# Three PSUM banks of one score tile become two tiles, in a chunked attention with two feed-forward layers

## The chip, the cores and the metric

The kernel runs on one core of one Trainium2 chip. The metric is device time in microseconds (us) of one execution; the median of several runs is given. The core has five engines with a queue of instructions each: TensorE (PE in the profile; PEld is its weight load), VectorE (DVE), ScalarE (ACT), GpSimd (POOL) and SyncE (SP, which here only issues DMAs). Each engine works its queue in order: an instruction that waits holds up all that stand behind it.

## The reference

Three stages follow each other on 3072 tokens (4 batches of 768), 512 channels wide:

- Attention in chunks: 8 heads of 64 channels. A chunk of 32 queries sees 8 memory keys and its own 32 keys with 16 before and 8 after, cut off at the ends of the sequence. Softmax, then the product with V.
- First feed-forward layer: `h = x @ w_in` (512 to 2048), `g = max(h, 0) + alpha * min(h, 0)`, `g @ w_out` back to 512.
- Second feed-forward layer of the same sizes with `g = h * sigmoid(1.702 h)`.

The weights of the two layers and their activations are worked on as a high and a low float16 half, so that one product takes three float16 matmuls.

## The kernel before

The tokens are cut into 12 blocks of 256 (`nb`), and each block into two halves of 128 queries (`i` = 0, 1). For blocks 2 to 11 the attention of one half goes through these steps, each a function in the code:

- `att_qk` (lines 476 to 483): the scores. For each of 8 heads two matmuls of 128x160 go into the PSUM tile `sps`, which is three banks of 512 float32: heads 0 to 2 in bank 0, heads 3 to 5 in bank 1, heads 6 and 7 in bank 2.
- `att_ext` (lines 485 to 504): ACT copies the band that each chunk needs out of `sps` into the SBUF tile `sc`: one copy of the memory columns (line 497) and one for each of four groups of 32 partitions (line 499). For blocks 2 to 11 each copy takes all three banks at once, as nine heads, the ninth being empty space.
- `att_smax`, `att_exp`, `att_sum`, `att_a16`: softmax on DVE, ACT and POOL, and the split of the probabilities into two float16 halves.
- `att_ta` (line 535): a transposing DMA from the SP queue makes `aT`.
- `att_pv` (lines 537 to 549): the product with V, 48 small matmuls (128x32, line 548). Half 0 writes bank 0 of `sps`, half 1 writes bank 1.
- `att_xhi` (ACT, line 129) and `att_xlo` (DVE, line 132) read that bank and write the high and the low half of `xt`, the input of the first feed-forward layer.

Blocks 0 and 1 do the scores in float32 (`att_qk32`, line 407); for them `att_ext` already has two parts, and their product with V goes to another PSUM pool.

The first layer works on pairs of 128 hidden channels: a group of 24 matmuls of line 580 (`mlp_g1`, reads `xt`) and a group of 24 of line 660 (`mlp_g2`). From about 200 us on these alternate on PE, 192 of each to a block, and the attention of the coming block is strewn between them. The plan `ATT` gives each attention step of a block its place in half steps of this loop; but what is written there is only the order in which the program is recorded. A scheduler, which follows the dependencies and its own estimates of durations, then fixes the order on each engine, and puts in the waits between engines. It keeps count of who wrote and who read a tile.

The second layer (lines 591 and 674) begins at about 724 us and uses no attention tile; `w2_open` closes the pool of `sps` and puts three other PSUM tiles in its place.

Of the kernel before, what the change touches and what calls it, by code (L numbers as in the profile page):

```python
# [8 lines left out]
F32 = mybir.dt.float32  # L9
# [17 lines left out]
F32B = (0, 1)  # L27
# [9 lines left out]
def kernel(  # L37
# [14 lines left out]
    nc = tc.nc  # L52
    B, H, S, D = q.shape
# [7 lines left out]
    HP = H // 2  # L61
    WIN = LEFT + CH + RIGHT
    SL = WIN + NM
# [3 lines left out]
    TW = BAND + NM  # L67
# [210 lines left out]
    att = {}  # L278

    def geo(nb):  # L280
        b, j = divmod(nb, S // TB)
        return b, j * TB

    def eng(nb):
        return nc.vector if nb == 0 else nc.gpsimd
# [112 lines left out]
    def att_qk32(nb, i):  # L398
        qt, kt = att["q", nb], att["k", nb]
        k0 = 0 if i == 0 else NM + 128  # L400
        for h in range(H):
            j, a = divmod(h, 2)
            if j < HP - 1:
                o, r, w = sps[:, a, j * TW:j * TW + TW], slice(a * D, a * D + D), qt[a * D:a * D + D, i, j]
            else:
                o, r, w = sps[:, 2, a * TW:a * TW + TW], slice(0, 2 * D), qz[:, i, a]
            nc.tensor.matmul(out=o, lhsT=w, rhs=kt[r, j, k0:k0 + TW], start=True, stop=True)

    def att_xmax(nb, i):
# [66 lines left out]
    def att_qk(nb, i):  # L476
        q1, q2 = att["q", nb]
        kt = att["k", nb]
        k0 = 0 if i == 0 else NM + 128
        for h in range(H):  # L480
            o = sps[:, h // 3, h % 3 * TW:h % 3 * TW + TW]
            nc.tensor.matmul(out=o, lhsT=q1[:, i, h], rhs=kt[:, h, k0:k0 + TW], start=True, stop=False)
            nc.tensor.matmul(out=o, lhsT=q2[:, i, h], rhs=kt[:, h, k0:k0 + TW], start=False, stop=True)

    def att_ext(nb, i):
        sc = at_p.tile([128, 9, SL], F32, tag="sc", name="sc", bufs=2)
        b, t0 = geo(nb)
        t1 = t0 + 128 * i
        sv = sc.rearrange("p (a b) s -> p a b s", a=3)
        pv = sps[:, :, 0:3 * TW].rearrange("p a (b t) -> p a b t", b=3)  # L490
        mo = 0 if i == 0 else BAND
        bo = NM if i == 0 else 0
        parts = [(sv, pv)]
        if nb in F32B:
            parts = [(sc[:, 0:6].rearrange("p (b a) s -> p a b s", a=2), pv[:, 0:2]), (sc[:, 6:8], pv[:, 2, 0:2])]
        for d, x in parts:
            nc.scalar.copy(d[..., WIN:SL], x[..., mo:mo + NM])
            for c in range(4):
                nc.scalar.copy(d[32 * c:32 * c + 32, ..., 0:WIN], x[32 * c:32 * c + 32, ..., bo + CH * c:bo + CH * c + WIN])  # L499
        if t1 == 0:  # L500
            eng(nb).memset(sc[0:32, 0:H, 0:LEFT], NEG)
        if t1 + 128 == S:
            nc.gpsimd.memset(sc[96:128, 0:H, WIN - RIGHT:WIN], NEG)
        att["s", nb, i] = sc[:, 0:H]

    def att_smax(nb, i):
        sc = att["s", nb, i]
# [30 lines left out]
    def att_pv(nb, i):  # L538
        aT = att.pop(("a", nb, i))
        if i == 0:  # L540
            xt[nb] = xt_p.tile([128, 2, KT, TB], F16, tag="xt", name="xt")
        xp = sps[:, i].rearrange("p (j t) -> p j t", j=HP)
        for j in range(HP):
            for c in range(4):
                o = xp[:, j, 32 * c:32 * c + 32]
                w = vbd[:, 4 * i + c, j].rearrange("p a (d t) -> p (a d) t", t=2)
                for n, (wt, a) in enumerate(((0, 0), (1, 0), (0, 1))):
                    nc.tensor.matmul(out=o, lhsT=w[:, :, wt], rhs=aT[:, a, j, 32 * c:32 * c + 32], start=(n == 0), stop=(n == 2))  # L548
        att["xp", nb, i] = xp
# [282 lines left out]
    def run_plan(t):  # L832
# [12 lines left out]
        (14, att_hi, 2), (15, att_lo, 2), (16, att_vw), (13, att_swap),  # L845
        *[(17 + h // 2, att_vr, h) for h in range(H)],
        (18, att_qk, 0), (18, att_ext, 0), (20, att_smax, 0), (21, att_qk, 1), (21, att_ext, 1),
        (22, att_exp, 0), (23, att_smax, 1), (24, att_sum, 0), (25, att_exp, 1), (26, att_a16, 0),
        (27, att_sum, 1), (28, att_ta, 0), (29, att_a16, 1), (31, att_ta, 1),
        (32, att_pv, 0), (33, att_xhi, 0), (34, att_xlo, 0), (34, att_pv, 1), (35, att_xhi, 1), (36, att_xlo, 1),  # L850
    ]
    for nb in range(3, NB):
# [3 lines left out]
    def split(m, p):  # L856
# [4 lines left out]
        (-103, zero_k), (-100.91, att_load, 0, 1), (-98.84, att_load, 0, 0), (-96.77, att_t32, 0),  # L861
        (-96.06, zero_v), (-95.87, alpha_load), (-95.35, att_load, 1, 0), (-90.2, w_load, 0, 1),
        (-89.08, alpha_prep), (-85.94, att_qk32, 0, 0), (-84.86, w_load, 0, 0), (-82.33, att_v32, 0, 1),
        (-78.47, w_load, 1, 0), (-74.28, w_max, 0, 0), (-68.89, att_ext, 0, 0), (-58.71, att_qk32, 0, 1),
        (-54.62, att_ext, 0, 1), (-47.58, att_smax, 0, 0), (-45.32, att_exp, 0, 0), (-41.66, att_sum, 0, 0),
        (-34.37, w_all, 0, 0, 1), (-33.6, w_max, 0, 1), (-31.58, w_scale, 0, 0, 1), (-28.74, att_v32, 0, 0),
        (-28.07, att_load, 1, 1), (-27.6, att_smax, 0, 1), (-26.72, w_all, 0, 1, 2), (-25.47, att_exp, 0, 1),
# [9 lines left out]
        (-7.61, w_dec_a, 0, 2), (-7.5, w_dec_b, 0, 2), (-7.25, w_dec_b, 0, 1), (-7.2, w_load, 1, 5),  # L877
        (-6.9, w_max, 0, 4), (-6.52, att_max, 2, 0), (-6.51, att_xlo, 0, 1), (-5.97, w_max, 1, 1),
        (-5.96, att_qk32, 1, 0), (-4.67, w_split_a, 0, 1), (-4.66, w_max, 1, 0), (-3.68, att_max, 2, 2),
        (-2.76, att_max, 2, 1), (-2.32, w_dec_a, 0, 3), (-2.14, w_split_a, 0, 2), (-1.65, w_split_b, 0, 1),  # L880
        (-1.25, att_ext, 1, 0), (-1.23, att_smax, 1, 0), (-0.54, att_exp, 1, 0), (-0.03, att_sum, 1, 0),
# [9 lines left out]
        (8.68, att_lo, 2, 2), (8.89, att_tq, 2), (8.99, w_first), (9.35, w_dec_b, 1, 0),  # L891
        (9.5, att_xlo, 1, 0), (9.66, att_xhi, 1, 1), (9.8, att_vw, 2), (9.83, w_dec_a, 1, 3),
        (10.76, att_swap, 2), (10.94, att_qk, 2, 0), (11.19, att_xlo, 1, 1), (11.28, att_vr, 2, 1),
        (12.17, w_max, 0, 6), (13.48, w_load, 0, 7), (13.76, att_ext, 2, 0), (14.12, w_dec_b, 1, 1),
        (14.26, att_smax, 2, 0), (14.44, w_dec_b, 1, 3), (14.78, att_vr, 2, 7), (14.88, w_max, 0, 5),
        (15.48, att_exp, 2, 0), (15.76, w_max, 0, 7), (16.07, w_split_a, 1, 1), (16.29, att_qk, 2, 1),
        (16.29, att_sum, 2, 0), (17.48, att_ext, 2, 1), (18.83, w_split_b, 1, 1), (18.86, att_smax, 2, 1),
        (18.99, att_vr, 2, 5), (19.25, w_all, 0, 4, 6), (19.27, w_split_a, 1, 0), (20.02, w_max, 1, 5),
# [4 lines left out]
        (25.09, att_vr, 2, 2), (25.62, w_split_b, 1, 0), (26.74, att_ta, 2, 0), (26.89, w_scale, 0, 6, 8),  # L903
        (27.59, att_a16, 2, 1), (28.18, w_load, 1, 4), (29.46, w_max, 1, 4), (29.5, w_split_a, 0, 4),
        (29.59, att_pv, 2, 0), (30.52, w_scale, 1, 4, 6), (30.65, att_ta, 2, 1), (31.18, w_dec_a, 0, 7),
        (31.7, w_split_b, 1, 2), (31.87, att_xhi, 2, 0), (32.19, att_pv, 2, 1), (33.03, w_dec_a, 0, 6),
        (33.15, w_split_b, 0, 4), (33.67, w_dec_b, 0, 7), (33.84, w_dec_b, 0, 6), (34.16, att_xhi, 2, 1),
        (34.77, w_split_a, 0, 6), (35.75, att_xlo, 2, 1), (35.88, att_xlo, 2, 0), (36.25, w_dec_b, 0, 5),
# [10 lines left out]
    for g in range(NP):  # L919
        m, p = 2 + g % 2, g // 2  # L920
        t = 24 * (g + 3) - 8 + EX3
# [12 lines left out]
    for b in range(NB):  # L934
        t = 3 * ((NP * (b + 1) if b >= NA else HF * (NA + b + 1)) + L0) + 2 - 3
# [7 lines left out]
    for sb in range(NB // 2):  # L943
        t = Q0 + 48 * sb
# [3 lines left out]
        t = 48 * sb + 80 if sb else 101.5  # L948
# [3 lines left out]
        if sb == NB // 2 - 1:  # L952
            t = Q0 + 20
# [8 lines left out]
    ps_s = l1.enter_context(tc.tile_pool(name="ps_s", bufs=1, space=PSUM))  # L962
    w_p = l1.enter_context(tc.tile_pool(name="wdec", bufs=2))
    at_1 = l1.enter_context(tc.tile_pool(name="at1", bufs=1))
    at_p = l1.enter_context(tc.tile_pool(name="at", bufs=1))
# [2 lines left out]
    vf = at_1.tile([128, 3, H, D], F32, name="vf")  # L968
    vbd = at_1.tile([128, 8, HP, 2, 2 * D], F16, name="vbd")
    lazy["yl_p"] = w_p  # L970
    sps = ps_s.tile([128, 3, 512], F32, name="sps")
    pend = []
    act = []

# [43 lines left out]
    qz = ident[:, 0:512].rearrange("p (i a t) -> p i a t", i=2, a=2)  # L1018
    ident = eye
    nc.vector.memset(wv, 0.0)  # L1020
    nc.vector.memset(sps[:, 2], 0.0)
    nc.scalar.activation(out=wv[:, 8:9], in_=wv[:, 7:8], func=ACTF.Exp)
    run_plan(0)
    for s in range(STEPS + EX):
# [3 lines left out]
    for q in range(STEPS // 2 + LQ):  # L1028
        t = Q0 + 6 * q
# [21 lines left out]
        if xs:  # L1051
            sb, p = divmod(q, NP)
# [33 lines left out]
```

## Time and profile before

| | |
|---|---|
| median of 3 runs | 1192.45 us (1189.9 to 1194.58) |
| profiled execution, first to last instruction | 1188.6 us |
| PE busy | 1079.9 us (91%) |
| DVE, POOL, ACT busy | 854.5 (72%), 639.9 (54%), 633.0 us (53%) |
| DMA queue with nearly all bytes | 51.0% of 16 engines |

The page of the profiled execution gives its span and no other time of its own; the median of the runs is 3.85 us above that span. The span falls into a start, in which PE is busy about three quarters of the time (up to some 200 us), the first layer with the attention beside it (to 724 us) and the second layer, in which PE hardly ever stops. A row of the timeline has start and duration in us, engine, line, operation, output and inputs with their shapes, the count of instructions merged into it, and in brackets how long the engine stood idle before it and what ended that.

### The profile page before, as it was taken

How to read it: one execution, taken by the hardware profiler on the slowest of the kernel's cores; microseconds unless marked ns; L12 is line 12 of the kernel's file. 1: busy time of each engine (PE TensorE's matmuls, PEld its weight loads, DVE VectorE, ACT ScalarE, POOL GpSimd, SP SyncE). 2: the span in 40 equal slices, each digit the busy share in tenths (PEclk: the TensorE clock that was granted, in tenths of full speed). 3: DMA queues.
4: the chain of work that ended last, by engine and by line, in shares of the span. 5: the costliest groups of instructions: out<-in, count | busy, mean ns of one | idle time of the engine just before them, and what ended most of it. 6: DMA issues, size and time to landing. Idle time of an engine off the chain costs nothing.

```text
span 1188.6 us, 25661 instructions
## 1 busy us (share of the span) xinstructions
PE 1079.9 (91%) x10294; PEld 957.4 (81%) x10294; DVE 854.5 (72%) x1509; ACT 633.0 (53%) x968; POOL 639.9 (54%) x740
## 2 busy tenths in 40 slices
PE   4676788988989898999799999989999999999998
PEld 3665677977878787888698988878888888888887
DVE  6899995659778777858797634787676767667662
ACT  4567455556666476656665632545444444443442
POOL 1244542218666456617572811787685676666672
PEclk9668998999999899999899999999999999999999
DMA  9969328576999678888966380640110202000001
GB/s 203 308 126 194 90 72 172 83 145 180 228 219 257 136 203 172 229 151 197 191 184 139 108 345 19 266 170 19 58 41 6 76 19 80 20 6 14 19 19 37
DMA packets 250536, 154.53 MB, mean 130 GB/s; under 512 B 201200, under 2 KB 221680, under 8 KB 249392
## 3 DMA queue, kind: packets, MB, share of 16 engines
q1 hardware_dynamic: 250416, 152.88, 51.0%
q8 instruction: 81, 1.33, 0.5%
q14 instruction: 39, 0.32, 0.1%
HBM read 91.96 MB, written 38.93 MB: 110 GB/s over the span
## 4 chain that ended last, share of the span: by engine, by line
PE 50%; DVE 20%; DMA 11%; POOL 5%; issue 5%; ACT 5%; SPq 3%; ACTq 0%; POOLq 0%; DVEq 0%
PE acc L674 17%; PE x L591 16%; PE h L580 8%; PE acc L660 7%; DVE g L132 3%; DVE gf L618 2%; DMA q<-q 2%; POOL ga L625 2%; DVE wmax L126 2%; DMA wbig<-in_moe_w_in_dram 2%; DVE wr L200 1%; DMA kf<-in_k_dram 1%; DMA qf<-in_q_dram 1%; DMA w<-in_moe_w_in_dram 1%; DVE wr L201 1%
## 5 line engine op out<-in xcount | busy, mean ns | idle before, releaser
L625 POOL TENSOR_TENSOR ga<-ga 128x128 f32<-128x128 f32 x384 | 213.2, 580 | 172.2 <-DVE ga L623 160.1
L580 PE MATMUL h<-xt,wbig 128*128 128x256 f16 x2304 | 280.7, 280 | 21.0 <-ACT xt L129 15.0
L660 PE MATMUL acc<-g,wbig 128*128 128x256 f16 x2304 | 279.9, 279 | 13.1 <-DVE gf L618 6.2
L580 PEld LDWEIGHTS <-wbig 128*128 128x128 f16 x2304 | 230.9, 100 | 53.9 <-issue 22.6
L660 PEld LDWEIGHTS <-wbig 128*128 128x128 f16 x2304 | 229.3, 100 | 44.3 <-DVE gf L618 7.3
L674 PE MATMUL acc<-w2o,g 128*128 128x256 f16 x2016 | 231.6, 274 | 4.2 <-ACT g L129 3.4
L591 PE MATMUL x<-yt,w2i 128*128 128x256 f16 x2016 | 229.9, 273 | 0.9 <-DVE ha L601 0.9
L674 PEld LDWEIGHTS <-g 128*128 128x128 f16 x2016 | 197.4, 98 | 29.1 <-ACT g L129 4.4
L591 PEld LDWEIGHTS <-w2i 128*128 128x128 f16 x2016 | 197.4, 98 | 24.1 <-issue 1.1
L132 DVE SCALAR_TENSOR_TENSOR g<-ga,gk,g 128x896 f16<-128x896 f32 x96 | 121.1, 1267 | 91.0 <-ACT g L129 90.7
L129 ACT ACTIVATE g<-ga,gk 128x896 f16<-128x896 f32 x96 | 98.9, 1037 | 96.0 <-POOL ga L625 87.1
L618 DVE SCALAR_TENSOR_TENSOR gf<-t,oma,h 128x256 f32<-128x256 f32 x192 | 83.4, 472 | 75.0 <-ACT t L615 74.9
L615 ACT ACTIVATE t<-h 128x512 f32<-128x512 f32 x96 | 56.7, 591 | 66.8 <-PE h L580 38.8
L132 DVE SCALAR_TENSOR_TENSOR g<-gf,gk,g 128x512 f16<-128x512 f32 x81 | 77.8, 960 | 17.0 <-ACT g L129 16.7
L808 POOL TENSOR_TENSOR o<-o 128x256 f32<-128x256 f32 x77 | 74.4, 980 | 10.0 <-ACT o L803 9.5
L622 ACT ACTIVATE ga<-ha,l2t 128x512 f32<-128x512 f32 x48 | 34.4, 718 | 80.7 <-DVE ha L603 80.7
L230 POOL TENSOR_TENSOR wt<-wr 128x512 f32<-128x512 f32 x16 | 24.0, 1500 | 81.2 <-DVE wr L207 59.0
L216 POOL TENSOR_TENSOR wbig<-wr,wbig 128x1024 f16<-128x1024 f32 x16 | 35.5, 2229 | 53.4 <-ACT wbig L211 53.4
L129 ACT ACTIVATE g<-gf,gk 128x512 f16<-128x512 f32 x81 | 57.7, 712 | 0.5 <-DVE gf L618 0.4
L499 ACT COPY sc<-sps 32x504 f32<-32x504 f32 (+2 forms) x112 | 56.3, 502 | 1.0
L623 DVE SCALAR_TENSOR_TENSOR ga<-ga,ha 128x512 f32<-128x512 f32 x48 | 35.6, 742 | 21.0 <-ACT ga L622 21.0
L548 PEld LDWEIGHTS <-vbd 128*128 128x128 f16 x960 | 27.2, 99 | 28.7 <-issue 18.4
(194 smaller groups left out, 1521.9 us busy)
## 6 DMA issues: line engine op xcount, KB each, us to landing
yt_dr<-yh SPq DMA_DIRECT2D x42, 256.0 KB
yt<-yt_dr SPq DMA_DIRECT2D x42, 256.0 KB
w<-in_moe_w_in_dram SPq DMA_DIRECT2D x10, 1024.0 KB
w<-in_moe_w_out_dram SPq DMA_DIRECT2D x10, 1024.0 KB
vbd<-v_dr SPq DMA_DIRECT2D x80, 112.0 KB
w2i_dr<-wh SPq DMA_DIRECT2D x28, 256.0 KB
w2o_dr<-wh SPq DMA_DIRECT2D x28, 256.0 KB
w2i<-w2i_dr SPq DMA_DIRECT2D x4, 1792.0 KB
```

What stands on the lines that cost most here:

```text
L129: return nc.scalar.activation(out=hi, in_=src, func=ACTF.Copy, scale=s)
L132: return nc.vector.scalar_tensor_tensor(out=lo, in0=src, scalar=s, in1=hi, op0=ALU.mult, op1=ALU.subtract)
L499: nc.scalar.copy(d[32 * c:32 * c + 32, ..., 0:WIN], x[32 * c:32 * c + 32, ..., bo + CH * c:bo + CH * c + WIN])
L580: nc.tensor.matmul(out=hp[:, e], lhsT=w[:, wt, o:o + 128], rhs=x[:, xh, kk], start=(n == 0), stop=(n == 3 * KT - 1))
L591: nc.tensor.matmul(out=xs[bank][:, i], lhsT=w[:, o, wt, kk * 256 + c:kk * 256 + c + 128], rhs=yt[sb, yi][:, yh, kk], start=(n == 0), stop= ...
L615: nc.scalar.activation(out=t, in_=hp, func=ACTF.Relu, scale=-1.0)
L618: nc.vector.scalar_tensor_tensor(out=g[:, e], in0=t[:, e], scalar=oma[:, f:f + 1], in1=hp[:, e], op0=ALU.mult, op1=ALU.add)
L623: nc.vector.scalar_tensor_tensor(out=t, in0=t, scalar=1.0, in1=hp, op0=ALU.add, op1=ALU.mult)
L625: nc.gpsimd.tensor_tensor(out=g[:, out_], in0=g[:, x], in1=g[:, y], op=op)
L660: nc.tensor.matmul(out=acc[layer, b][dt // 2][:, dt % 2 * TB:(dt % 2 + 1) * TB], lhsT=w[:, wt, dt * 128:(dt + 1) * 128], rhs=g16[:, gh, e] ...
L674: nc.tensor.matmul(out=acc[layer, b][bank][:, i * 256:(i + 1) * 256], lhsT=g16[:, gh, gs], rhs=w[:, o, wt, p % 2], start=(p == 0 and n == ...
L808: e.tensor_tensor(out=ov[:, out_], in0=ov[:, x], in1=ov[:, y], op=op)
```

## The change

The tile `sps` of three banks becomes `sc01` (two banks: heads 0 to 5) and `sc2` (one bank: heads 6 and 7). The copies out of the scores come in two parts for every block, six heads and two heads, and `sc` holds eight heads in place of nine. The product with V of half 0 writes the first bank of `sc01`, that of half 1 writes `sc2`. The memset of the third bank at the start goes, since no copy reads its empty columns any more.

```diff
@@ att_qk32
-                o, r, w = sps[:, a, j * TW:j * TW + TW], slice(a * D, a * D + D), qt[a * D:a * D + D, i, j]
+                o, r, w = sc01[:, a, j * TW:j * TW + TW], slice(a * D, a * D + D), qt[a * D:a * D + D, i, j]
             else:
-                o, r, w = sps[:, 2, a * TW:a * TW + TW], slice(0, 2 * D), qz[:, i, a]
+                o, r, w = sc2[:, a * TW:a * TW + TW], slice(0, 2 * D), qz[:, i, a]
@@ att_qk
-            o = sps[:, h // 3, h % 3 * TW:h % 3 * TW + TW]
+            o = sc01[:, h // 3, h % 3 * TW:h % 3 * TW + TW] if h < 6 else sc2[:, (h - 6) * TW:(h - 5) * TW]
@@ att_ext
-        sc = at_p.tile([128, 9, SL], F32, tag="sc", name="sc", bufs=2)
+        sc = at_p.tile([128, H, SL], F32, tag="sc", name="sc", bufs=2)
...
-        sv = sc.rearrange("p (a b) s -> p a b s", a=3)
-        pv = sps[:, :, 0:3 * TW].rearrange("p a (b t) -> p a b t", b=3)
+        p01 = sc01[:, :, 0:3 * TW].rearrange("p a (b t) -> p a b t", b=3)
+        p2 = sc2[:, 0:2 * TW].rearrange("p (b t) -> p b t", b=2)
...
-        parts = [(sv, pv)]
-        if nb in F32B:
-            parts = [(sc[:, 0:6].rearrange("p (b a) s -> p a b s", a=2), pv[:, 0:2]), (sc[:, 6:8], pv[:, 2, 0:2])]
+        s01 = sc[:, 0:6].rearrange("p (b a) s -> p a b s", a=2) if nb in F32B else sc[:, 0:6].rearrange("p (a b) s -> p a b s", a=2)
+        parts = [(s01, p01), (sc[:, 6:8], p2)]
@@ att_pv
-        xp = sps[:, i].rearrange("p (j t) -> p j t", j=HP)
+        xp = (sc01[:, 0] if i == 0 else sc2).rearrange("p (j t) -> p j t", j=HP)
@@ set-up
-    sps = ps_s.tile([128, 3, 512], F32, name="sps")
+    sc01 = ps_s.tile([128, 2, 512], F32, name="sc01")
+    sc2 = ps_s.tile([128, 512], F32, name="sc2")
...
-    nc.vector.memset(sps[:, 2], 0.0)
```

The scheduler orders the whole program anew, so rows move on every engine. On PE, this is where the product with V of half 1 begins in block 7, before the change (a name with `_49` is the counter that a row waits for; `acc` and line 660 are the first layer):

```order
L660 LDWEIGHTS wbig
L660 MATMUL acc<-g_5650,wbig 128x256
L548 LDWEIGHTS vbd [waits DMAHW4_49]
L548 MATMUL sps<-aT,vbd 128x32 [waits DVE_49]
L548 LDWEIGHTS vbd
```

Here is the same place after the change, where `sc_165` is `sc2` and every line below the attention has a number one lower:

```order
L659 LDWEIGHTS wbig
L659 MATMUL acc<-g_5607,wbig 128x256
L547 LDWEIGHTS vbd
L547 MATMUL sc_165<-aT,vbd 128x32 [waits DMAHW5_49]
L547 LDWEIGHTS vbd
```

The first matmul waited for DVE, and now waits for a DMA only; between the two halves there stood 53 matmuls of the first layer, and now 24. In block 9 it is 53 and 24 as well, in the other blocks 26 to 37 and now 24, but for block 4 with 48 before and after. The first matmuls of line 580 that read a block's `xt` come 49 matmuls of the first layer after half 1 (37 in block 4, before and after); before, it was 36 to 46.

On DVE, this is the stretch from the first `xt` row of block 7 to its second, before the change (`g`, `gf` and `t` belong to the first layer, `v` to the attention of the next block, `ar` to a weight's maximum):

```order
L132 SCALAR_TENSOR_TENSOR xt<-sps,xt 128x4x128 [waits Activation_49]
L618 SCALAR_TENSOR_TENSOR gf<-t,oma,h 128x256 [waits Activation_49]
L618 SCALAR_TENSOR_TENSOR gf<-t,oma,h 128x256
L132 SCALAR_TENSOR_TENSOR g_5976<-gf,gk_145,g_5976 128x512 [waits DVE_49,Activation_49]
L132 SCALAR_TENSOR_TENSOR v_5973<-vf,blk_140,v_5973 128x1536 [waits DMAHW7_49,DMAHW6_49,DMAHW0_49]
L122 TENSOR_REDUCE ar<-mx 128x1 [waits PE_49]
L132 SCALAR_TENSOR_TENSOR xt<-sps,xt 128x4x128 [waits Activation_49]
```

And this is the same stretch after the change:

```order
L132 SCALAR_TENSOR_TENSOR g_5960<-gf,gk_145,g_5960 128x512 [waits Activation_49]
L132 SCALAR_TENSOR_TENSOR xt<-sc_164,xt 128x4x128 [waits Activation_49]
L132 SCALAR_TENSOR_TENSOR xt<-sc_165,xt 128x4x128 [waits Activation_49]
L617 SCALAR_TENSOR_TENSOR gf<-t,oma,h 128x256 [waits Activation_49]
L617 SCALAR_TENSOR_TENSOR gf<-t,oma,h 128x256
L122 TENSOR_REDUCE ar<-mx 128x1 [waits PE_49]
```

The two `xt` rows now stand next to each other, with the first layer's work behind both. On ACT three casts of line 759 stand between the two `xt` rows of this block after the change; before there were eight rows.

## Rows read from the trace of the kernel before

**Rows 1.** Page, busy time of each engine, share of span, instructions.

```profile
PE 1079.9 (91%) x10294; PEld 957.4 (81%) x10294; DVE 854.5 (72%) x1509; ACT 633.0 (53%) x968; POOL 639.9 (54%) x740
```

**Rows 2.** Busy time by stretch: length, PE, PEld, DVE, ACT, POOL, PEclk, DMA, GB/s.

```profile
0.00:103.00 103.00, 63.76 (x382) 54.86 (x383) 84.92 (x178) 55.61 (x97) 32.39 (x30) 0.75 0.92 215
103.00:200.00 97.00, 80.45 (x777) 70.13 (x776) 84.37 (x147) 56.08 (x80) 41.84 (x23) 0.96 0.47 109
200.00:724.00 524.00, 481.42 (x5001) 427.67 (x5002) 371.80 (x673) 312.77 (x494) 265.70 (x215) 0.96 0.76 183
```

**Rows 3.** Waits of PE, 200 to 724 us: total us, times, longest.

```profile
PE sps L548 <- DVE xt L132: 17.8, 5, 4.1
PE sps L548 <- DMA aT<-a: 6.4, 2, 4.6
...
PE h L580 <- ACT xt L129: 3.1, 2, 2.0
PE sps L482 <- ACT sc L499: 2.9, 3, 1.3
```

**Rows 4.** Timeline of block 5 around its product with V.

```profile
341.20 1.36 PE L548 MATMUL sps<-aT,vbd 128*128 128x32 f16 x48
342.25 1.36 SPq L535 DMA_TRANSPOSE aT<-a  x1
...
342.41 2.78 PE L660 MATMUL acc<-g,wbig 128*128 128x256 f16 x24
...
345.02 1.58 PE L580 MATMUL h<-xt,wbig 128*128 128x256 f16 x13
...
349.56 0.68 DVE L132 SCALAR_TENSOR_TENSOR xt<-sps,xt 128x512 f16<-128x512 f32 x1
...
350.29 1.45 PE L548 MATMUL sps<-aT,vbd 128*128 128x32 f16 x48 [3.68 <-DVE xt L132]
...
351.57 2.40 PE L580 MATMUL h<-xt,wbig 128*128 128x256 f16 x11
```

**Rows 5.** Timeline of blocks 6 and 8, the transposing DMA and half 1.

```profile
401.42 1.29 SPq L535 DMA_TRANSPOSE aT<-a  x1
...
404.62 0.10 PEld L548 LDWEIGHTS <-vbd 128*128 128x128 f16 x1 [3.00 <-DMA aT<-a]
...
405.83 1.44 PE L548 MATMUL sps<-aT,vbd 128*128 128x32 f16 x48 [3.93 <-DVE xt L132]
...
513.62 1.29 SPq L535 DMA_TRANSPOSE aT<-a  x1
...
517.29 1.44 PE L548 MATMUL sps<-aT,vbd 128*128 128x32 f16 x48 [1.87 <-DMA aT<-a]
```

**Rows 6.** Timeline of block 7.

```profile
453.96 1.35 PE L548 MATMUL sps<-aT,vbd 128*128 128x32 f16 x48
...
463.21 0.57 ACT L129 ACTIVATE xt<-sps 128x512 f16<-128x512 f32 x1
...
464.72 0.61 ACT L759 CAST yh<-yf 128x512 f16<-128x512 f32 x1
...
465.24 1.37 PE L548 MATMUL sps<-aT,vbd 128*128 128x32 f16 x48 [4.13 <-DVE xt L132]
...
466.45 3.85 PE L660 MATMUL acc<-g,wbig 128*128 128x256 f16 x19
...
474.44 1.03 PE L580 MATMUL h<-xt,wbig 128*128 128x256 f16 x8 [1.08 <-ACT xt L129]
```

**Rows 7.** Groups by line and form, ACT, copies of the scores: busy us, mean ns.

```profile
L499 ACT COPY sc<-sps 32x504 f32<-32x504 f32 x80 | 45.5, 569 | 0.7
L499 ACT COPY sc<-sps 32x336 f32<-32x336 f32 x16 | 6.9, 429 | 0.1
...
L499 ACT COPY sc<-sps 32x112 f32<-32x112 f32 x16 | 3.9, 242 | 0.2
...
L497 ACT COPY sc<-sps 128x16 f32<-128x16 f32 x4 | 0.7, 173 | 0.0
```

More of the change, by code (lines that the diff above doesn't have):

```diff
@@ L503, in att_ext @@
             nc.gpsimd.memset(sc[96:128, 0:H, WIN - RIGHT:WIN], NEG)
-        att["s", nb, i] = sc[:, 0:H]
+        att["s", nb, i] = sc
     def att_smax(nb, i):
```

## The prediction

> **What bounds the kernel now.** I read the page's busy times first: PE is busy for 91% of the span, DVE for 72% [rows 1], so the question is where PE is not busy, and whether the change touches those places. The table of busy time by stretch answers the first half. Up to 103 us PE has 63.8 of 103 us and DVE 84.9; from 103 to 200 us PE has 80.5 and DVE 84.4 of 97: the start is held by DVE and by loads. From 200 to 724 us PE has 481.4 of 524 us, DVE 371.8, ACT 312.8 [rows 2]: here PE is the bound, and 43 us of it are lost. After 724 us no instruction of the changed tiles runs. So the change can act on the start and on this middle stretch.
>
> The waits of PE in the middle stretch name the losses: 17.8 us in five waits of the product with V (line 548) for DVE's `xt` rows, 6.4 us in two waits of the same line for the transposing DMA that makes `aT`, 3.1 us of the first layer (line 580) for `xt`, and 2.9 us of the scores (line 482) for the copies out of them [rows 3]. All four are waits around the tile that is cut.
>
> The timeline of block 5 shows the mechanism. Half 0 of the product with V starts at 341.20; PE then does first-layer work until 346.6 and stands for 3.68 us, and half 1 starts at 350.29, when DVE's `xt` row of half 0 (349.56, 0.68 long) has ended [rows 4]. Half 1 writes another bank than the one DVE reads. Its wait is there because both banks belong to one tile, and the program's order shows it: half 1 carried a wait for DVE, and in the changed program carries only one for a DMA.
>
> **The change part by part.** The sum is made against the profiled execution (span 1188.6 us); the median of the runs is 3.85 us above that, and I add this to its result.
>
> 1. *The wait of half 1 for DVE goes.* What is late next is `aT` of half 1, and the place of half 1 moves too: in the changed order it stands 24 first-layer matmuls behind half 0 (block 4 keeps its 48). A half takes 1.21 us on PE and 24 matmuls 2.61 (341.20 to 342.41 to 345.02 [rows 4]), so PE reaches it 3.8 us after half 0 began. The DMA lands 3.2 us after its issue in block 6 (401.42 to 404.62) and 3.7 in block 8 (513.62 to 517.29) [rows 5].
>    - Block 5: issue 342.25, landing 345.5 to 345.9; PE arrives at 345.0. A wait of 0.6 is left of 3.68.
>    - Block 6: PE arrives 11 matmuls (1.36) earlier than it did, at 400.5, and the DMA lands at 404.62 [rows 5]: 4.1 instead of 3.93, a loss of 0.15.
>    - Block 8: PE arrives at 514.1 instead of 515.4, and the DMA lands at 517.29 as before: a loss of 1.35.
>    - Blocks 7, 9 and 10, the rest of the five waits: there the timeline has the DMA issued before half 0 starts, so it has landed. Their whole waits go.
>    - So 17.8 less block 6's 3.93 is 13.9 gained [rows 3, 5], and 0.6, 0.15 and 1.35 lost again.
>
> 2. *The slow matmuls behind those waits.* In block 5 the 11 matmuls after the wait take 2.40 us; at the pace of the 24 in 2.78 [rows 4] they would take 1.36. In block 7, 19 take 3.85 instead of 2.23 [rows 6]. After such a standstill PE runs for a while at the lower of its two clocks. I take the smaller figure, 1.0 us, for each of the four waits that vanish: 4.0 gained.
>
> 3. *The first layer's wait for `xt`.* The 3.1 us [rows 3] lie in blocks 7 and 9. In block 7 `xt` of half 1 was made only when half 1, started at 465.24, had been worked off by an ACT queue with eight rows in between, and line 580 stood until 474.44 [rows 6]. That goes. But PE now comes earlier to the same place: 453.96 plus 1.21, 2.61, 1.21 and 49 matmuls of 0.109 (2.61 over 24) is 464.3. ACT's first `xt` row runs at 463.21 and the third of the casts behind it ends at 465.33 [rows 6]; then the second `xt` row (0.57) and DVE's (0.68, [rows 4]) make it ready at 466.6. Less the four matmuls that need only the high half (0.44), PE waits 1.9 us. For blocks 7 and 9, which run alike, that is 3.8 in place of 3.1: a loss of 0.7. This new wait is the one to look for.
>
> 4. *The copies out of the scores.* One copy of 504 columns (569 ns) becomes one of 336 (429) and one of 112 (242); four of these per half are 0.41 us more, and the second copy of the memory columns (173 ns) makes it 0.58 [rows 7]. Twenty halves give 11.6 us more of ACT, which is busy for 313 of 524 us [rows 2]. Most of it lies beside PE's work. It shows where the chain from the scores to `aT` is what PE waits for: blocks 4, 6 and 8, 0.58 each, 1.75 lost. In return the first six heads' banks are free before the last two are copied; that can shorten the 2.9 us of line 482 [rows 3], but the last two heads then wait for the longer whole, so I take nothing for it.
>
>    The Trainium skill, "ScalarE: Activation LUTs", section "What ACT_TABLE_LOAD costs", puts an activation with immediates at 186 ns plus 0.833 ns a column, with 93 ns of overlap between neighbours. By that the extra cost would be an estimated 0.27 us a half and 5.4 us in all, and the loss in blocks 4, 6 and 8 0.8 instead of 1.75. The rows have the same slope (187 ns for 224 columns) but a base of 149 ns [rows 7]; the sum stays with the rows.
>
> 5. *The memset at the start* is one DVE instruction before the first loads land. DVE has 18 us without work up to 103 us [rows 2], which hide it. Nothing.
>
> 6. *The new order elsewhere.* The start is re-ordered too: the trace cannot price it. Bounds from the nearest rows: DVE has 31 us without work up to 200 us [rows 2], and a third of that, 10 us, is the most that I would give to a better order; as large a loss bounds the other side. I take zero, because the same DVE work stands there.
>
> Sum: 13.9 + 4.0 gained, less 0.6 + 0.15 + 1.35 (part 1), 0.7 (part 3) and 1.75 (part 4): 13.4 us. The span becomes 1175.2, the median 1179.0.
>
> **The rivals.**
>
> *The DMA waits go as well.* `aT` lands late in blocks 4, 6 and 8 because of work queued on ACT, POOL and SP in front of it, and this order changes too; scores and copies may also overlap where they could not. Then the 6.4 us [rows 3], block 6's 3.93, and the 3.85 us of losses from parts 1 and 4 are won back, except block 5's 0.6: 13.6 more, 1165. Against it: nothing in the changed code shortens that chain, and its copies get longer.
>
> *The wait only moves.* ACT and DVE, not PE, set when `xt` is ready: in block 7 ACT's first `xt` row starts 8.0 us after half 0 has ended its 1.21 [rows 6]. If their rows are really driven by their own queues, PE arrives earlier and stands before line 580 in all four blocks for about 3 us more than in my sum: 12 less, 1191. For it: DVE is at 71% and ACT at 60% of the stretch [rows 2]. Against it: in block 5 both have done the row of half 0 by 350.24, and half 1 needs about 0.7 more, while PE comes to line 580 at 345.7 + 1.2 + 5.3 = 352.2.
>
> *Slower: the longer copies set the pace.* If the chain from the scores over `aT` to half 1 is what paces every block, each block pays 2 × 0.58 us and the removed wait turns into one for `aT`: ten blocks, 11.6 us, 1204. The point from which this decides is that `aT` of half 1 lands after PE's arrival in most blocks. Now it does in three of ten (4, 6, 8), and a little in block 5; in the others the DMA is issued before half 0 starts, so 1.2 us more would not reach it.
>
> **How the numbers follow.** My forecast, with a range of its own of 1171 to 1186, gets 0.50; the larger gain (1165) 0.15; the moved wait (1191) 0.22; the longer copies (1204) 0.13. About 0.5% (6 us) is what a measurement of this kernel can tell from no change, so faster means under 1186.5 and slower over 1198.4. Faster takes 0.48 of the first case, all of the second and 0.05 of the third: 0.68. Slower takes 0.11 of the last and 0.01 of the third: 0.12. The rest, 0.20, is no change. The range of 1164 to 1196 takes in the first three cases with part 6's bounds on the forecast, and leaves out the slower one and the far end of the larger gain.
>
> **What would show it.** In the profile after: PE's waits of the product with V for DVE's `xt` are gone (17.8 to 0), those for the DMA rise from 6.4 to about 13 (blocks 4, 6, 8 and a little in 5); line 580 waits about 2 us for `xt` in blocks 7 and 9; the copies of 32x336 and 32x112 have 80 more instructions each at about 430 and 240 ns; PE's busy time up to 200 us is about what it was; the second layer begins some 13 us earlier. The prediction is wrong if the start to 200 us has moved by more than 5 us, if the DMA waits vanish or spread to blocks 7, 9 and 10, or if waits of line 580 for `xt` add up to more than 8 us.

## The result, and the profile after

The changed kernel takes 1200.9 us (median of 4 runs, 1199.63 to 1201.89), the kernel before 1191.18 on the same chip: a ratio of 1.0082, 95% interval 1.0062 to 1.0101. It is 0.8% slower; 1179 was predicted, and faster. The profiled execution spans 1199.0 us, 10.4 more than before.

Line numbers of the changed kernel are one lower than before's around the attention (548 becomes 547, 580 becomes 579). The page's busy times answer to [rows 1]:

```profile
PE 1083.9 (90%) x10294; PEld 958.7 (80%) x10294; DVE 848.8 (71%) x1508; ACT 641.2 (53%) x1068; POOL 637.0 (53%) x740
```

The work is the same but for 100 more instructions on ACT and one memset fewer on DVE. By stretch (length; PE, PEld, DVE, ACT, POOL; granted clock; DMA share; GB/s), beside [rows 2]:

```profile
0.00:103.00 103.00, 62.55 (x388) 53.59 (x389) 84.38 (x179) 57.60 (x104) 38.90 (x31) 0.72 0.89 209
103.00:200.00 97.00, 81.22 (x743) 69.44 (x741) 81.20 (x142) 53.93 (x80) 36.01 (x21) 0.88 0.51 118
200.00:724.00 524.00, 475.34 (x4940) 421.51 (x4939) 366.63 (x670) 318.32 (x581) 261.80 (x216) 0.96 0.76 183
```

The start did move, but it is not where the time is lost. Up to 200 us PE is busy for 143.8 us, 144.2 before, yet from 103 to 200 us at a granted clock of 0.88 in place of 0.96, and it gets 28 matmuls less far. By the count of line 580's (now 579's) matmuls the first layer is 5.6 us behind at 190 us. By 244 us it is 0.3 us ahead: the kernel before waited there 4.1 us for a load of q, and the changed kernel does not. Nor does the second layer lose anything. Its first rows, before and after, are

```profile
724.50 1.25 PE L591 MATMUL x<-yt,w2i 128*128 128x256 f16 x10
```

```profile
734.91 1.25 PE L590 MATMUL x<-yt,w2i 128*128 128x256 f16 x10
```

and from there to the end it is 464.1 us in both. So the 10.4 us arise between 244 us and the start of the second layer. From 200 to 724 us PE does 6 us less. The waits of PE there (total, times, longest), beside [rows 3]:

```profile
PE sc L482 <- ACT sc L498: 10.8, 3, 5.7
PE acc L659 <- DVE gf L617: 9.5, 3, 5.4
PE sc L547 <- DMA aT<-a: 7.8, 2, 4.6
PE h L579 <- DVE gf L617: 7.4, 2, 3.8
```

The 17.8 us that the product with V waited for `xt` are gone to the last. But the sum of all rows of this view is 48.2 us against 44.4 before. Waits that were small or absent have grown: the scores for the copies of the half before (2.9 to 10.8), the first layer for DVE's `gf` (0 to 7.4).

Block 5 on PE, where [rows 4] had the wait of 3.68 us:

```profile
343.67 1.35 PE L547 MATMUL sc<-aT,vbd 128*128 128x32 f16 x48
344.87 2.78 PE L659 MATMUL acc<-g,wbig 128*128 128x256 f16 x24
347.49 1.35 PE L547 MATMUL sc<-aT,vbd 128*128 128x32 f16 x48
348.69 2.78 PE L579 MATMUL h<-xt,wbig 128*128 128x256 f16 x24
```

No wait, and no slow matmuls behind it. The same holds in blocks 6, 7, 8 and 9. In block 7, beside [rows 6]:

```profile
457.69 1.35 PE L547 MATMUL sc<-aT,vbd 128*128 128x32 f16 x48
...
461.51 1.35 PE L547 MATMUL sc<-aT,vbd 128*128 128x32 f16 x48
...
468.18 2.78 PE L579 MATMUL h<-xt,wbig 128*128 128x256 f16 x24
...
477.13 1.05 PE L579 MATMUL h<-xt,wbig 128*128 128x256 f16 x8 [3.55 <-DVE gf L617]
```

Half 0 starts 3.7 us later than before and half 1 3.7 us earlier (461.51 for 465.24). The group of the first layer that begins at 468.18 is, by the count of these matmuls, the one that began at 474.44 [rows 6]: PE is 6.2 us ahead. At the next group it stands for 3.55 us, and 48 of these matmuls further on it is 0.3 us behind the kernel before (483.5 for 483.2). What it waited for is on ACT:

```profile
474.11 1.48 ACT L331 ACTIVATE junk<-kf 128x1536 f16<-128x1536 f32 x1 [6.29 <-DMA kf<-in_mem_k_dram]
...
475.59 0.58 ACT L614 ACTIVATE t<-h 128x512 f32<-128x512 f32 x1
476.07 2.05 ACT L129 ACTIVATE v<-vf,blk 128x1536 f16<-128x1536 f32 x1
477.98 0.70 ACT L129 ACTIVATE g<-gf,gk 128x512 f16<-128x512 f32 x1
```

and on DVE:

```profile
476.20 0.87 DVE L617 SCALAR_TENSOR_TENSOR gf<-t,oma,h 128x256 f32<-128x256 f32 x2 [8.20 <-ACT t L614]
```

`junk<-kf` is the maximum of the k of block 9 (`att_max`), and it waits 6.29 us for that k to be loaded. Behind it in ACT's queue stand `t`, the split of v and `g`; DVE stands 8.20 us for `t`, and PE for DVE. In the kernel before, `t`, v and `g` stood ahead of this maximum:

```profile
466.76 2.06 ACT L129 ACTIVATE v<-vf,blk 128x1536 f16<-128x1536 f32 x1
468.69 0.70 ACT L129 ACTIVATE g<-gf,gk 128x512 f16<-128x512 f32 x1
472.32 1.48 ACT L331 ACTIVATE junk<-kf 128x1536 f16<-128x1536 f32 x1 [2.94 <-DMA qf<-in_q_dram]
```

So the scheduler, with one dependency less, has also put other rows in another order. The same three rows stand behind the maximum for block 11, which waits 5.99 us (until 589.3); behind that for block 8, which waits 7.88 us (until 419.59), only `g` does. Block 10 shows another place, on ACT:

```profile
628.85 1.57 ACT L129 ACTIVATE k<-kf,blk 128x1536 f16<-128x1536 f32 x1 [4.94 <-DVE blk L112]
630.33 1.13 ACT L129 ACTIVATE q<-qf,blk 128x1024 f16<-128x1024 f32 x1
631.37 0.60 ACT L527 CAST a<-sc 128x512 f16<-128x512 f32 x1
```

and on PE:

```profile
630.54 1.35 PE L547 MATMUL sc<-aT,vbd 128*128 128x32 f16 x48
...
637.68 1.35 PE L547 MATMUL sc<-aT,vbd 128*128 128x32 f16 x48 [3.15 <-DMA aT<-a]
```

The cast of half 1's probabilities stands behind two casts for block 11 that wait 4.94 us for a scale; in the kernel before it stood ahead of them. `aT` is late by it, and half 1 waits 3.15 us.

The copies, beside [rows 7], cost what was read there (line, form, count, busy us, mean ns):

```profile
L498 ACT COPY sc<-sc 32x336 f32<-32x336 f32 x96 | 41.2, 429 | 0.8
L498 ACT COPY sc<-sc 32x112 f32<-32x112 f32 x96 | 23.2, 242 | 0.9
```

Reading alone leaves three causes for 10 us: the copies, the new order, or a wait that was slack. The experiments part them.

### The profile page after: what moved, and what is told of

Same layout as the page of the kernel before. It is cut to its first block, busy times and chain, and to the rows that moved or that the text cites. A ratio compares the mean times of both kernels' runs of the same rounds, so it can differ in the third digit from the quotient of the medians.

```text
span 1199.0 us, 25751 instructions
## 1 busy us (share of the span) xinstructions
PE 1083.9 (90%) x10294; PEld 958.7 (80%) x10294; DVE 848.8 (71%) x1508; ACT 641.2 (53%) x1068; POOL 637.0 (53%) x740
## 4 chain that ended last, share of the span: by engine, by line
PE 44%; DVE 22%; DMA 12%; ACT 6%; issue 5%; POOL 5%; SPq 5%; ACTq 0%; POOLq 0%; DVEq 0%
PE acc L673 17%; PE x L590 16%; PE acc L659 5%; PE h L579 5%; DVE g L132 3%; DVE gf L617 3%; DMA qf<-in_q_dram 2%; DVE wr L201 2%; SPq L318 2%; DVE wmax L126 2%; DMA vf<-in_v_dram 2%; POOL ga L624 2%; DMA kf<-in_k_dram 1%; DVE blk L126 1%; DMA w<-in_moe_w_in_dram 1%
## 5 line engine op out<-in xcount | busy, mean ns | idle before, releaser
L498 ACT COPY sc<-sc 32x336 f32<-32x336 f32 (+1 forms) x192 | 64.4, 336 | 1.8
L216 POOL TENSOR_TENSOR wbig<-wr,wbig 128x1024 f16<-128x1024 f32 x16 | 38.3, 2403 | 46.0 <-DMA kf<-in_k_dram 26.1
L241 POOL TENSOR_TENSOR wh<-wt,wh 128x512 f16<-128x512 f32 x32 | 42.9, 1349 | 11.9 <-ACT wh L240 11.7
```

The lines of the kernel that those rows point to most:

```text
L241: nc.gpsimd.tensor_tensor(out=hv[:, 1], in0=src, in1=hv[:, 0], op=ALU.subtract)
```

## The experiments

Two theories to begin with. C: the longer copies set the pace, and the removed wait was slack. O: the loss is the new order. To hold them apart, the order must not change when the tiles do. Same-engine edges without a semaphore do that: at the end of the program each engine's instructions are chained in a given order.

```diff
+    def hold(order):
...
+        for e, runs in order.items():
+            prev = None
+            seq = [own[e][j] for s, n in runs for j in range(s, s + n)]
+            for x in seq:
+                if prev is not None:
+                    tc.add_manual_dep(x, prev.name, ...
+                prev = x
```

`own[e]` is what engine `e` was given, `order` the wanted sequence as stretches of positions in it. Below, "old order" (`OLD`) is that of the kernel before, "new order" (`NEW`) that of the changed kernel. Where single rows are moved, a fence lists rows of an engine's queue by output and input: + where a row stands now, - where it stood. Block numbers in experiments 9, 11, 12, 14 and 15 are those of the k and q whose maxima stand there, elsewhere those of the product with V. Ratios are to the kernel before on the same chip, with 95% intervals; the medians of different experiments come from different chips, so it is the ratios that are compared. Lines of held kernels are two higher than in the program without it. The changed kernel held in its own order with nothing moved was not run; experiments 5 and 12 come closest to it.

**1 to 4: tiles, copies and order apart.**

1, changed tiles and copies, old order.

```diff
+    hold(OLD)     # on the changed kernel
```

> The changed tiles and the changed copies, but every engine's instructions held in the order of the kernel before (the five extra copies of a half stand right behind the five old ones). Theory C (the longer copies set the pace; the removed wait was slack, which the next block's attention chain used up anyway): 1201 us, within 3, as the changed kernel. Theory O (the loss comes from the new order of the loads, maxima, scalings and casts of the next block): no slower than 1192; and if the 17.8 us of waits for xt were more than slack, 1178 to 1186. In both, no wait of the product with V for DVE's xt is left.

Measured: 1191.38 us, 0.9995 (0.9985 to 1.0004). Against the changed kernel's 1.0082 the same instructions in the other order are 0.87%, some 10 us, faster, and the two intervals lie far apart. The loss is the order.

2, one tile, old order, copies in two parts.

```diff
-        parts = [(sv, pv)]
...
+        s01 = ... if nb in F32B else sv[:, 0:2]
+        parts = [(s01, pv[:, 0:2]), (sc[:, 6:8], pv[:, 2, 0:2])]
+    hold(OLD)
```

> The kernel before with its single score tile and its order on every engine; only the copies out of the scores come in two parts for every block (0.58 us more of ACT a half, 11.6 us in all). Theory C: 1200 to 1203 us. Theory O: 1191 to 1194.

Measured: 1193.96 us, 1.0012 (1.0000 to 1.0024), as O expected. The 11.6 us of copies cost 1.4 us (0 to 2.9).

3, changed kernel, new order, one copy in place of five for the last two heads.

```diff
+            if nb not in F32B and x is p2:
+                nc.scalar.copy(d, x[..., 0:SL])
+                continue
+    hold(NEW)
```

> The changed kernel in its own order on every engine, but the five copies of the last two heads are one copy of 128x2x64 for blocks 2 to 11, which takes the wrong columns: that part of the softmax is left wrong. By the copy rows (149 ns and 0.833 ns a column) it takes 0.26 us in place of 1.14, so a half costs ACT 0.88 us less than in the changed kernel and 0.30 less than in the kernel before. Theory C: the loss of 10 us goes and a little more, 1183 to 1191 us. Theory O: 1197 to 1201.

Measured: 1199.08 us, 1.0055 (1.0038 to 1.0072). With 17.6 us less of copies than the changed kernel it is 0.27% (3 us) faster and still slow: O.

4, the same cheap copy in the old order.

> The changed tiles with the one cheap copy for the last two heads (wrong columns, as in the third run), held in the order of the kernel before. Theory C: 1181 to 1189 us, 12 to 18 below the first run. Theory O: within 4 us of the first run, both no slower than 1192.

Measured: 1188.18 us, 0.9955 (0.9940 to 0.9970): 0.40%, 4.8 us, below experiment 1. That is a little more than O allowed and far from the 12 to 18 us of C, though the time itself lies in C's range too. Copies cost here between about an eighth and a quarter of their length.

C is dead as the cause of the loss. But its second half lives: between experiments 2 and 1 only the tiles differ (order and copies are the same), and they are worth 0.17%, 2 us, just clear of the noise, where a wait of 17.8 us went. Where it went, PE's waits of experiment 1 tell:

```profile
PE h L581 <- ACT xt L131: 16.7, 3, 7.3
PE acc L661 <- DVE gf L619: 7.6, 4, 5.1
PE sc L484 <- ACT sc L500: 7.5, 3, 3.8
```

17.8 us of the product with V have become 16.7 us of the first layer for ACT's `xt`. Block 7 on PE:

```profile
466.95 1.35 PE L549 MATMUL sc<-aT,vbd 128*128 128x32 f16 x48
...
480.74 1.87 PE L581 MATMUL h<-xt,wbig 128*128 128x256 f16 x8 [7.29 <-ACT xt L131]
```

Half 1 is done at 468.2, and `xt` of half 1 is made at 480.11, because in ACT's queue the maximum of block 9's k stands in front of it and waits for its load until 478.62. All rows of this view together are 46.3 us, 44.4 in the kernel before: PE stands as long as it did, at other rows.

**5 to 7: where the new order loses.** Theory P: in one place, the cast of block 10. Theory S: spread.

5, changed kernel, new order but for two rows.

```diff
@@ ACT, block 10, half 1
+a<-sc
 k<-kf,blk
 q<-qf,blk
-a<-sc
@@ SP
+aT<-a
 kt<-k
-aT<-a
```

> The changed kernel in its own order on every engine, but for two rows of block 10, half 1: ACT casts the probabilities to float16 ahead of the two casts of the next block's k and q, which wait for DVE's scale, and SP issues the transposing DMA of aT ahead of that of kt. Theory P (this one place is where the new order loses): the wait of 3.15 us for aT goes, and the 24 matmuls behind it that took 4.45 us take 2.78, so 1200.9 becomes 1194 to 1198. Theory S (the loss is spread; whatever is early is held up at the next place): 1199 to 1201.

Measured: 1198.87 us, 1.0052 (1.0034 to 1.0071): between the two, nearer to S. Some 3 us of the 10 lie here, hardly more than the noise.

6, new order up to the first scores of block 10, then the old (`hold(NEW up to there + OLD)`).

> The changed kernel, in its own order up to the first scores of block 10 (about 596 us), and in the order of the kernel before from there. Theory P (the new order loses in blocks 10 and 11 only): 1188 to 1193 us. Theory S (spread over the blocks): 1196 to 1200.

Measured: 1199.41 us, 1.0067 (1.0050 to 1.0083): S. 7, the complement.

> The complement: the changed tiles in the order of the kernel before up to the first scores of block 10, and in the changed kernel's order from there. Theory P: 1198 to 1203 us. Theory S: 1191 to 1194.

Measured: 1195.07 us, 1.0025 (1.0014 to 1.0036), between P and S. Against experiment 1 the new order costs 0.72% before block 10 and 0.30% from there.

**8 to 11: is a wait that goes time that is won?**

8, experiment 1 with `xt` of half 1 moved ahead of the row that held it, in blocks 7 and 9.

```diff
@@ ACT, blocks 7 and 9
+xt<-sc        (half 1)
 junk<-kf
-xt<-sc
@@ DVE
+xt<-sc,xt
 v<-vf,blk,v
-xt<-sc,xt
```

> The first run (changed tiles, order of the kernel before) with four rows moved: in blocks 7 and 9 ACT makes xt of half 1 ahead of the maximum of the next block's k, which waits for a load, and DVE makes its xt of half 1 ahead of the split of v. In the first run PE stood 7.29 and 7.05 us there. Theory W (those waits are the gain that was missed): about 4.5 us less in each block, 1180 to 1185. Theory L (the next block's attention chain, not PE, sets the pace here, and PE's lead is given back at its scores or its product with V): 1188 to 1192.

Measured: 1193.68 us, 1.0011 (1.0001 to 1.0020). Theory W is wrong: the time did not fall. Theory L's range ends 1.7 us below it. PE's waits:

```profile
PE sc L484 <- ACT sc L500: 14.6, 4, 6.6
PE acc L661 <- DVE gf L619: 10.0, 5, 4.1
...
PE h L581 <- ACT xt L131: 3.5, 3, 1.7
```

The wait for `xt` fell from 16.7 to 3.5 us, that for the copies rose from 7.5 to 14.6; all rows together are 44.4 us, as in the kernel before. Where PE's lead ends can be seen at the next scores. Experiment 1, first scores of block 8 on PE, then the first copy on ACT:

```profile
488.20 0.23 PE L484 MATMUL sc<-kt,q 128*128 128x160 f16 x1
...
491.30 0.19 ACT L498 COPY sc<-sc 128x48 f32<-128x48 f32 x1
```

Experiment 8:

```profile
481.15 0.23 PE L484 MATMUL sc<-kt,q 128*128 128x160 f16 x1
...
490.94 0.60 ACT L616 ACTIVATE t<-h 128x512 f32<-128x512 f32 x1 [3.33 <-DVE gf L619]
491.44 0.71 ACT L131 ACTIVATE g<-gf,gk 128x512 f16<-128x512 f32 x1
492.05 0.19 ACT L498 COPY sc<-sc 128x48 f32<-128x48 f32 x1
```

The scores come 7.05 us earlier, their copies 0.75 us later. ACT gets to them only when it has worked off its queue, which waited for a load, for a store and for DVE. The second half's scores then wait for the copies, 6.59 us, and the lead is gone.

9, experiment 8 with ACT's maxima of blocks 7 to 11 moved behind the casts and scalings that follow them.

```diff
@@ ACT, block 9 (11 alike; in 7, 8 and 10 past t, g, yh and wr)
-junk<-kf
-junk<-qf
 yh, yh, yh, wr, wr
+junk<-kf
+junk<-qf
```

> The fourth run of the second series (changed tiles, order of the kernel before, xt ahead of the maximum of k), and in blocks 7 to 11 ACT's maxima of the next block's k and q, which stood 22.2 us in waits for their loads, moved four to six rows back, behind the casts and scalings that stand ahead of the next copies out of the scores. Theory Q (ACT's queue, standing before these loads, sets the pace of the stretch, so PE's early products gained nothing): 10 to 22 us less, 1171 to 1184. Theory R (the pace comes from elsewhere in the chain, such as the scale on DVE or the loads' issue): 1188 to 1195.

Measured: 1189.60 us, 0.9974 (0.9963 to 0.9985): 4 us of 22, in R's range. But ACT's standing has not gone with the loads. Its waits from 330 to 600 us in experiment 8:

```profile
ACT junk L333 <- DMA qf<-in_q_dram: 15.2, 6, 6.3
...
ACT junk L333 <- DMA kf<-in_mem_k_dram: 6.5, 2, 3.6
...
ACT yh L760 <- DMA yt_dr<-yh: 2.5, 2, 1.3
```

and in experiment 9:

```profile
ACT yh L760 <- DMA yt_dr<-yh: 19.6, 3, 6.8
...
ACT junk L333 <- DMA qf<-in_q_dram: 0.2, 1, 0.2
```

The rows that came to the front, the casts `yh`, now wait for a store. So this says little against Q. 10, the same with one tile and one-part copies.

> The same moved rows on ACT and DVE, with the single score tile and the one-part copies of the kernel before. Theory Q: faster than before too, but the waits of the product with V for DVE's xt now count: 4 to 12 us slower than the kernel with two tiles and the same rows moved, 1178 to 1192. Theory R: 1188 to 1193, within 3 us of the kernel with two tiles.

Measured: 1189.64 us, 0.9970 (0.9958 to 0.9982): R, for Q asked 4 to 12 us more than experiment 9. There is again no difference between one tile with one-part copies and two tiles with two-part copies. 11, the same move in the new order with experiment 5's rows.

> The fifth kernel (changed kernel, its own order, one cast and one DMA of block 10 earlier), with the maxima of k and q of blocks 7 to 11 moved back in the same way where the program allows it (two maxima of k in blocks 9 and 11 stay). Theory Q: 1180 to 1192 us, at least 7 less than the 1198.9 of the fifth kernel. Theory R: 1196 to 1200.

Measured: 1193.11 us, 1.0002 (0.9991 to 1.0014). By the ratios it is 0.50%, 6 us, below experiment 5, between Q and R. In the old order the same move brought 0.37%; the noise does not tell the two apart.

**12 to 15: the rows that lose, and a better version.** Only the rows of k that the new order had put ahead of `t`, v and `g` are moved back in 12; 13 adds experiment 5's.

```diff
@@ ACT, blocks 9 and 11 (block 8: past g alone)
-junk<-kf
 t<-h
 v<-vf,blk
 g<-gf,gk
+junk<-kf
 junk<-qf
```

> The changed kernel in its own order, but in blocks 8, 9 and 11 ACT's maximum of the next block's k, which the new order put ahead of the first layer's rows (of g alone in block 8, of t, v and g in blocks 9 and 11) and which stood 7.88, 6.29 and 5.99 us before its load, goes back behind them, where the kernel before has it. Theory K (these rows are the new order's loss before block 10): the two waits of the first layer for gf behind them (3.55 and 3.81 us) go, and the scales of blocks 9 and 11 come 4 and 2.5 us earlier: 4 to 7 us less, 1194 to 1197. Theory S (spread over many rows): 1198 to 1201.

Measured: 1195.13 us, 1.0013 (1.0000 to 1.0026), as K expected: three rows of ACT are 0.69%, 6 to 8 us.

> The same, with the cast and the DMA of block 10 moved as in the fifth kernel (which gained 2 us). Theory K with theory P's two rows: 1190 to 1194, so that nearly the whole loss of the new order is found. Theory S: 1196 to 1199.

Measured: 1190.18 us, 0.9976 (0.9964 to 0.9988), as K expected, and faster than the kernel before. PE's waits:

```profile
PE sc L484 <- ACT sc L500: 16.5, 5, 4.8
PE acc L661 <- DVE gf L619: 7.8, 5, 4.3
...
PE sc L549 <- DMA aT<-a: 4.6, 1, 4.6
```

The first layer's 7.4 us for `gf` and block 10's 3.15 us for `aT` are gone; all rows together are 36.5 us in place of the changed kernel's 48.2. Here PE's standing did fall, and the time with it. The largest part of what is left, 16.5 us, are the scores that wait for the copies.

14, experiment 10 with three more casts of ACT, which in block 9 waited 7 us for stores, put behind the scalings and maxima.

```diff
@@ ACT, blocks 9 and 11
-yh, yh, yh
 wr, wr, junk, junk
+yh, yh, yh
```

> The tenth kernel (single tile, order of the kernel before, the maxima of k and q later), with the three casts that stood 7 us before stores of the same tensor in blocks 9 and 11 put behind the weights' scalings and the maxima. Theory R (the removed wait is taken up by the next queue, as each time before): 1187 to 1191. Theory Q (ACT's waits set the pace): 1178 to 1185.

Measured: 1188.24 us, 0.9956 (0.9939 to 0.9973): R. ACT's waits for stores of `yh` from 330 to 600 us fall from 16.9 us in experiment 10 to 3.6, but its rows `wr` now stand there for DVE (1.5 us in experiment 10):

```profile
ACT wr L196 <- DVE wcs L189: 10.7, 3, 4.9
```

15, experiment 13 with the maxima of experiment 9 moved behind as well.

> The thirteenth kernel (changed kernel, its own order, three maxima of k, one cast and one DMA moved back or forth: 0.24% faster than the kernel before), with the maxima of k and q of blocks 7 to 11 moved behind the casts and scalings ahead of the next copies as well, as in the ninth. Theory Q (the load waits of ACT are worth what they were in the old order): 3 to 5 us less, 1185 to 1188. Theory R (they only move): 1188 to 1191.

Measured: 1187.25 us, 0.9960 (0.9948 to 0.9972), in Q's range, but only 0.16% below 13, at the edge of the noise. Experiments 9, 10 and 13 to 15 beat both kernels. 14 and 15 cannot be told apart, one with the single tile, one with two.

## Why the prediction was wrong, step by step

The forecast was 1179 us and the result 1200.9. Two steps failed: the price of step 1 and the zero of step 6. Of the 22 us some 12 lie in steps 1 to 4, which promised 13.4 us and in the old order brought less than 1 (experiment 1), and some 10 in step 6.

*Step 1, the wait of half 1 for DVE goes (13.9 us net of block 6).* The wait went as foreseen, 17.8 to 0. Its price failed. At a fixed order and with equal copies the tiles give 2 us. The step priced a wait of PE as time, because PE was busy for 481 of 524 us [rows 2]. That figure says that PE has little slack over the stretch, not that it leads at this point of the block: in experiment 1 the standing came back at other rows, 46.3 us in all for 44.4. Of the waits for `aT` that the step foresaw in blocks 5, 6 and 8 none came; in block 5 half 0 itself was 2.5 us later (343.67 for 341.20 [rows 4]). One that the step ruled out came, 3.15 us in block 10, and such a spread was one of the prediction's own signs of being wrong.

*Step 2, slow matmuls (4.0).* Those behind half 1 are gone, but the granted clock of the stretch is 0.96 before and after: other standstills brought others, as in block 10, where 24 matmuls behind the wait of 3.15 us take 4.45 us in place of 2.78.

*Step 3, the first layer's new wait for `xt` (0.7 lost).* In the new order it is 1.3 us in all, in one block, less than was written. In the old order (experiment 1) it is 16.7 us in three blocks, 14.3 of it in blocks 7 and 9, where the maximum that waits for a load stands ahead of the second `xt` row; in the changed kernel's order it stands behind it. The rival "the wait only moves" named such a wait and 1191 us, and experiment 1 has both. But experiment 8 took most of that wait away and the time stayed, so this wait does not hold the end either. In the changed kernel PE was ahead, but its lead went into ACT's waits for the loads of k, which came no earlier (block 9's maximum starts at 474.11, before at 472.32).

*Step 4, the copies (1.75).* Right: 1.4 us measured in experiment 2, with an interval from 0 to 2.9. By the figures of the Trainium skill, "ScalarE: Activation LUTs", section "What ACT_TABLE_LOAD costs", the extra cost is an estimated 0.27 us a half. In the traces the copies of a half take 2.92 us in the changed kernel (610.21 to 613.13) and 2.41 in one part (487.63 to 490.04 in experiment 10). That is 0.51 us more, nearer to the rows' 0.58 than to 0.27, and neither size decides.

*Step 6, the new order elsewhere (0, bounded by 10 either way).* This is the step that turned the sign: 0.87%, some 10 us lost (experiment 1), at its bound, and not in the start, where the bound was taken from, but behind 200 us. The start moved by 5.6 us at 190 us, more than the 5 us that the prediction had named as a sign, and that was made up by 244 us. The reason given, that the same work stands there, was none: five rows of ACT and SP that changed places with their neighbours are 1.06%, 11 to 13 us (from the changed kernel to experiment 13). What could have been seen beforehand is the order of ACT around `junk<-kf`, a row that waits for a load in every block.

*The slower rival* named 1204 us. That it came near the time is luck: experiments 2 to 4 rule out its mechanism.

The Trainium skill, "Perfetto Trace Analysis", section "Optimization Strategy", tells to find the gaps of the most-contended engine and what blocks them. The prediction did just that. Here it does not suffice: gaps of PE vanished in experiments 1 and 8 (17.8 and 13.2 us), and the time stayed, because about as much standing came back at other rows.

What stays open is which loop sets the pace of the stretch. Taking away PE's waits of the product with V brings 2 us, moving ACT's waits for loads 4 us. But each time the standing came back at other rows (on PE in experiments 1 and 8, on ACT in 9 and 14), so that ACT's queue sets the pace is neither shown nor ruled out.

## What to carry to other kernels

A dependency that is taken away lets the scheduler put everything in another order, and the order may be worth more than the dependency: compare the engines' orders around every row that waits for a load, and hold the old order to measure the edit by itself. Before a wait is priced, follow the engine that ended it past that point, to the next row in its queue that waits for something else; if that row comes no earlier, the gain may end there. After the change, compare the sum of all waits, not only the one that went. Put a row that waits for a load behind the rows that have their inputs (0.69% in experiment 12), and look whether the row that comes to the front then waits in its place (experiments 9 and 14).

## What was not expected of the hardware

Nothing in the engines' own speeds. In the coupling of their queues: ACT is busy in the changed kernel for only 61% of the stretch (318 of 524 us) and waits for loads of q and k, yet 17.6 us more or less of copies on it move the end by no more than 3 to 5 us, and the 7 us by which PE's scores of block 8 come earlier in experiment 8 do not bring the copy that reads them forward at all.
